# Three of four mask products in bfloat16, and three products of zeros between the first two chunks' attention, in an mLSTM cell followed by a squared-ReLU FFN

## The chip, the cores and the metric

The kernel runs on one core of one Trainium2 chip. The metric is the device time of one launch, in microseconds (us); lower is better. TensorE is called PE in the profile, its weight loads PEld, VectorE DVE, ScalarE ACT, GpSimdE POOL, and SyncE, which issues most DMAs, SP.

## The reference, cut to what matters

```python
# q, k, v, o_gate: (4, 8, 768, 40); i_gate, f_gate: (4, 8, 768); w_in: (320, 2048); w_out: (2048, 320)
for t in range(S):
    m_new = maximum(f[t] + m, i[t])
    f_stab, i_stab = exp(f[t] + m - m_new), exp(i[t] - m_new)
    m = m_new
    C = f_stab * C + i_stab * outer(v[t], k[t])          # 40 x 40 for each head
    n = f_stab * n + i_stab * k[t]
    y[t] = sigmoid(o[t]) * (C @ q[t]) / maximum(abs(n @ q[t]), 1.0)
x = y.transpose(0, 2, 1, 3).reshape(3072, 320)           # tokens x (heads * head_dim)
out = square(maximum(x @ w_in, 0.0)) @ w_out             # w_in, w_out arrive as float64
```

## The kernel before, in words

The recurrence is computed in chunks of 128 tokens: a sequence has 6 chunks, the four sequences 24, and the chunks are numbered s = 0 to 23 through all of them. Within a chunk the states are replaced by a masked matrix. For each of the 8 heads there is a matrix W of 128 key tokens (partitions) by 128 query tokens, W = exp(A + b), where A is a running sum of log decays that depends on the query token, b depends on the key token, and where the key comes after the query the entry must be zero. `do_gates` computes the running sums with scans on DVE (A_sb, line 251, and i_sb, line 255). `turn_gates` transposes them on PE, and ACT copies them out (b_T and eA_T, line 262).

Chunks 0 and 1 get their A from PE, by `spread_A(s)`: for each of two halves of four heads, a product of the identity with a matrix `later` (zero, or -1e30 where key is after query; line 346, 128x512 for four heads at once) starts a PSUM tile, and four products of a selecting matrix `sel` with A_sb (line 350) add A, spread over all partitions. These first products are here called the mask products; there are four, (s, i) = (0, 0), (0, 1), (1, 0), (1, 1). All later chunks read A back from DRAM with a broadcasting DMA (`load_A`), and POOL masks it (`mask`, line 359).

A chunk goes through these steps. `transposes` (line 412) turns k and q on PE, and copies them out on ACT or DVE (line 415). `scores` (line 424) multiplies them. `weigh` makes W on ACT (line 383), the decay of the state `dec` (line 387), and values-times-weight `vw` on POOL (line 396). `weighted` multiplies scores and W on DVE (line 437, into P_sb, for chunk 1 into r_sb). `attend` issues on PE the share of the old state `hi` (line 446), the new state `dC` (line 453), and the weights' product with the values `hp` (line 460); these three come from a pool of three PSUM banks, so the `hp` of chunk 1 goes into the bank of the `hp` of chunk 0 and waits until that is read. DVE then adds and normalises (`sum_of_h`, `normalise`; line 601 is the last to read `hp` of chunk 0), `turn_rows` transposes the result x on PE (line 633) and ACT copies it to xT (line 634).

The FFN takes two chunks at a time: `ffn1_main` and `ffn1_rest` (lines 649 and 660) multiply xT with w_in, ACT takes the ReLU (line 675) and DVE the square (line 682), and a second set of products with w_out follows. The weights arrive as float64 and are rounded to float32 by `Rounding`: `words` on ACT (lines 195 and 197), `join` with three steps on DVE (lines 206, 210, 211) and one on POOL (line 215), 26 pieces in all, whose loads SP issues as pieces are done.

The order of all this is written out by hand: each engine executes its instructions in the order in which the source issues them. `idle(n)` issues n products of zeros (line 802: bfloat16, 128x512) into a bank that nobody reads. The stretch around the change is

```python
    attend(0)
    rounding.step()
    sum_of_h(0)
    normalise(0)
    mask(2)
    attend(1)
```

and ahead of it stand `idle(12)`, `transposes(0, apart=4)`, `idle(4)`, `scores(0)`, `idle(3)`, `do_gates()`, `spread_A(0)`, `turn_gates()`, two joins, `weigh(0)`, `transposes(1)`, `spread_A(1)`, `scores(1)`, `weigh(1)`, and `weighted` for both. The tiles of the masks (`later`, `sel`, `keep`) lie in a pool that is freed after `weigh(1)`.

Of the kernel before, what the change touches and what calls it, by code (L numbers as in the profile page):

```python
# [12 lines left out]
BF16 = mybir.dt.bfloat16  # L13
# [4 lines left out]
P = 128  # L18
# [11 lines left out]
def kernel(  # L30
# [27 lines left out]
    nc = tc.nc  # L58
# [29 lines left out]
    gates = first.enter_context(tc.tile_pool(name="gates", bufs=1))  # L88
# [17 lines left out]
    ident = consts.tile([P, P], F32)  # L106
    bdm = conv.tile([P, PR, 2, D1], F32, bufs=1)
    keep = gates.tile([BH, NB, P], F32)
    sel = gates.tile([BH, H, P], F32)
    later = gates.tile([P, P], F32)  # L110

    w_in = consts.tile([P, 2, DFF], F32)
    w_in2 = consts.tile([P, NPAIR, P], F32)
# [2 lines left out]
    def make_consts():  # L116
        for t in kq_b:
            nc.vector.memset(t[:, :, :, D:], 0.0)
        for t in va_b:
            nc.vector.memset(t[:, :, D:], 1.0)  # L120
        nc.vector.memset(keep[:], 1.0)
        nc.vector.memset(keep[:, :, 0:1], 0.0)
        make_identity(nc, ident[:])

        nc.gpsimd.memset(sel[:], 0.0)
        nc.gpsimd.affine_select(
            sel[:], sel[:], compare_op=ALU.not_equal, fill=1.0, base=0, pattern=[[-1, H], [0, P]], channel_multiplier=1,
        )

        nc.gpsimd.memset(later[:], 0.0)  # L130
        nc.gpsimd.affine_select(
            later[:], later[:], compare_op=ALU.is_ge, fill=-1e30, base=0, pattern=[[1, P]], channel_multiplier=-1,
        )

        nc.gpsimd.memset(bdm[:], 1.0)
        nc.gpsimd.memset(bdm[:DP, :, 1, :], 0.0)
        nc.gpsimd.memset(bdm[DP:, :, 0, :], 0.0)
        for t in va_w:
            nc.gpsimd.memset(t[:, H * D1 :], 0.0)
# [189 lines left out]
    def load_A(s):  # L329
        b, c = divmod(s, NB)  # L330
        d = st.setdefault(s, {})
        A = ld.tile([P, H, P], F32, name="A_bc", bufs=2)
        d["A"] = [A]
        nc.sync.dma_start(
            A[:], bass.AP(A_d.tensor, A_d.offset + b * H * S + c * P, [[0, P], [S, H], [1, P]]),
        )

    def spread_A(s):

        b, c = divmod(s, NB)  # L340
        H2 = H // 2
        d = st.setdefault(s, {})
        d["A"] = []
        for i in range(2):
            A = ps_h.tile([P, H2, P], F32, name="A_ps", tag="h_ps")
            nc.tensor.matmul(
                A[:], lhsT=ident[:], rhs=later[:].unsqueeze(1).to_broadcast([P, H2, P]), start=True, stop=False,
            )
            for h in range(H2):
                nc.tensor.matmul(  # L350
                    A[:, h, :], lhsT=sel[:, i * H2 + h, :], rhs=A_sb[:, c * P : (c + 1) * P],
                    start=False, stop=(h == H2 - 1),
                )
            d["A"].append(A)

    def mask(s):

        A = st[s]["A"][0]
        nc.gpsimd.affine_select(  # L359
            A[:], A[:], compare_op=ALU.is_ge, fill=-1e30, base=0, pattern=[[0, H], [1, P]], channel_multiplier=-1,  # L360
        )
# [77 lines left out]
    def attend(s):  # L439
        b, c = divmod(s, NB)  # L440
        d = st[s]
        C = st.get("C")
        if c > 0:
            hi = ps_at.tile([P, H, D1], F32, name="hi", tag="at")
            for j in range(PR):
                nc.tensor.matmul(
                    hi[:, 2 * j : 2 * j + 2, :].rearrange("p h d -> p (h d)"), lhsT=d["qT"][:, j, :],
                    rhs=C[:, j].rearrange("p h d -> p (h d)"), start=True, stop=True,
                )
        if c + 1 < NB:  # L450
            dC = ps_at.tile([P, PR, 2, D1], F32, name="dC", tag="at")
            for j in range(PR):
                nc.tensor.matmul(
                    dC[:, j].rearrange("p h d -> p (h d)"),
                    lhsT=d["kq"][:, 0, 2 * j : 2 * j + 2, :].rearrange("p h d -> p (h d)"),
                    rhs=d["vw"][:, 2 * j : 2 * j + 2, :].rearrange("p h d -> p (h d)"), start=True, stop=True,
                )
        hp = d["hp"] = ps_at.tile([P, H, D1], F32, name="hp", tag="at")
        for h in range(H):
            nc.tensor.matmul(  # L460
                hp[:, h, :], lhsT=d["P"][h % 2][:, h // 2, :], rhs=d["va"][:, h, :], start=True, stop=True,
            )
        d["num"] = hp
        if c > 0:
            num = d["num"] = old.tile([P, H, D1], F32, name="num", bufs=1)
            nc.vector.tensor_tensor(
                num[:], hi[:], eA_T[:, b, c, :].unsqueeze(2).to_broadcast([P, H, D1]), op=ALU.mult,
            )
        if c + 1 < NB:
            Cn = old.tile([P, PR, 2, D1], F32, name="C_sb")  # L470
            nc.vector.tensor_tensor(Cn[:], dC[:], bdm[:], op=ALU.mult)
            if c > 0:
                Cd = old.tile([P, H, D1], F32, name="Cd", bufs=1)
                nc.gpsimd.tensor_tensor(
                    Cd[:], C[:].rearrange("p j i d -> p (j i) d"),
                    d["dec"][:].unsqueeze(2).to_broadcast([P, H, D1]), op=ALU.mult,
                )
                Cf = Cn[:].rearrange("p j i d -> p (j i) d")
                nc.gpsimd.tensor_tensor(Cf, Cf, Cd[:], op=ALU.add)
            st["C"] = Cn  # L480
# [104 lines left out]
    def sum_of_h(s):  # L585
        d = st[s]
        num = d["num"]
        if num is not d["hp"]:
            nc.vector.tensor_tensor(num[:], num[:], d["hp"][:], op=ALU.add)

    def normalise(s):
        d = st[s]
        num = d["num"]
        dm = work.tile([P, H], F32, name="dm")
        nc.vector.tensor_scalar(dm[:], num[:, :, D], scalar1=-1.0, scalar2=1.0, op0=ALU.mult, op1=ALU.max)
        nc.vector.tensor_tensor(dm[:], dm[:], num[:, :, D], op=ALU.max)
        nc.vector.reciprocal(dm[:], dm[:])

        x = d["x"] = work.tile([P, 3 * P], F32, name="x_sb")
        x3 = x[:, :DM].rearrange("p (h d) -> p h d", d=D)  # L600
        nc.vector.tensor_tensor(x3, num[:, :, :D], d["og"], op=ALU.mult)
        nc.vector.tensor_tensor(x3, x3, dm[:].unsqueeze(2).to_broadcast([P, H, D]), op=ALU.mult)
        nc.vector.tensor_copy(x[:, DM:], x[:, DM - KR : DM])
# [195 lines left out]
    def idle(n):  # L799
        t = ps_h.tile([P, W], F32, name="idle", tag="h_ps")  # L800
        for _ in range(n):
            nc.tensor.matmul(
                t[:], lhsT=zeros[:, :1].to_broadcast([P, P]), rhs=zeros[:, :1].to_broadcast([P, W]), start=True, stop=True,
            )
# [12 lines left out]
    load_part(0, 1)  # L817
    fetch(2)
    make_consts()
    load_part(1, 0)  # L820
    load_part(1, 1)
# [12 lines left out]
    rounding.words()  # L834
    nc.scalar.dma_start(A_d[:, :], A_sb[:])
    spread_A(0)
    rounding.words()
    turn_gates()
    rounding.join()
    rounding.join()  # L840
    weigh(0)
    transposes(1, (False, True))
    spread_A(1)
    scores(1, (True, True))
    weigh(1)
# [14 lines left out]
    sum_of_h(0)  # L860
    normalise(0)
    mask(2)
    attend(1)
    sum_of_h(1)
    normalise(1)
# [15 lines left out]
    for u in range(8):  # L881
        s = 2 + u // 2
# [118 lines left out]
    for n, (which, g, i) in enumerate(parts):  # L1001
        s, at = 6 + n // 4, n % 4
# [200 lines left out]
```

## Time and profile before

| | |
|---|---|
| time, median of 3 runs | 521.13 us (519.98 to 521.82) |
| time of the profiled execution | 521.13 us |
| span of the profiled execution, first to last instruction | 519.3 us |
| mean granted TensorE clock | 0.990 |
| busy: PE, DVE, ACT, POOL | 511.1, 333.9, 194.3, 91.0 us |

All times inside the kernel are us from the span's start in the profiled execution. A float32 product appears in the profile as two records, so "x8" on line 350 is four products. A granted clock of 1.00 is full speed. A group's duration reaches from the start of its first to the modelled end of its last record; the spacing of starts shows what a product costs in a row of them.

### The profile page before, as it was taken

How to read it: one execution, taken by the hardware profiler on the slowest of the kernel's cores; microseconds unless marked ns; L12 is line 12 of the kernel's file. 1: busy time of each engine (PE TensorE's matmuls, PEld its weight loads, DVE VectorE, ACT ScalarE, POOL GpSimd, SP SyncE). 2: the span in 40 equal slices, each digit the busy share in tenths (PEclk: the TensorE clock that was granted, in tenths of full speed). 3: DMA queues.
4: the chain of work that ended last, by engine and by line, in shares of the span. 5: the costliest groups of instructions: out<-in, count | busy, mean ns of one | idle time of the engine just before them, and what ended most of it. 6: DMA issues, size and time to landing. Idle time of an engine off the chain costs nothing.

```text
span 519.3 us, 10359 instructions
## 1 busy us (share of the span) xinstructions
PE 511.1 (98%) x3933; PEld 450.2 (87%) x3933; DVE 333.9 (64%) x638; ACT 194.3 (37%) x460; POOL 91.0 (18%) x110
## 2 busy tenths in 40 slices
PE   9999899999999999999999999999999999999997
PEld 4778788886698898998898898998898898998997
DVE  8669987857895574674864865764864863431461
ACT  3867468434454423532334423235432301103000
POOL 3345643222321111010210211110110000000000
PEclk9989799999999999999999999999999999999999
DMA  9997599867867768876775685686664221200000
GB/s 193 243 232 155 157 169 202 206 144 140 177 133 170 138 156 161 159 150 143 174 144 116 170 151 115 162 142 138 157 145 75 65 68 48 66 0 1 27 27 25
DMA packets 239394, 68.06 MB, mean 131 GB/s; under 512 B 185744, under 2 KB 233872, under 8 KB 239344
## 3 DMA queue, kind: packets, MB, share of 16 engines
q1 hardware_dynamic: 239248, 67.20, 60.2%
q8 instruction: 31, 0.51, 0.4%
q10 hardware_dynamic: 96, 0.20, 0.1%
q14 instruction: 19, 0.16, 0.1%
HBM read 55.08 MB, written 17.86 MB: 140 GB/s over the span
## 4 chain that ended last, share of the span: by engine, by line
PE 72%; DVE 2%; DMA 2%; issue 2%; SPq 1%; ACT 0%; DVEq 0%
PE h_ps L743 30%; PE h_ps L649 24%; PE h_ps L660 7%; PE numT L534 3%; PE tp L424 3%; PE h_ps L689 3%; PE numT L523 2%; DMA num_rows<-tn 1%; PE numT L512 1%; SPq L562 1%; DVE g L682 0%; DVE mag L210 0%; SPq L618 0%; DMA xT<-x_rows 0%; DMA kq<-num_rows 0%
## 5 line engine op out<-in xcount | busy, mean ns | idle before, releaser
L649 PE MATMUL h_ps<-xT,w_in 128*128 128x256 f32 x768 | 172.9, 383 | 1.4 <-ACT xT L634 0.6
L649 PEld LDWEIGHTS h_ps<-xT,w_in 128*128 128x128 f32 x768 | 144.4, 191 | 23.2 <-issue 1.4
L675 ACT ACTIVATE r_sb<-h_ps 128x512 f32<-128x512 f32 x96 | 50.5, 598 | 108.6 <-PE h_ps L660 52.9
L682 DVE TENSOR_TENSOR g<-r_sb 128x512 f32<-128x512 f32 x96 | 68.5, 762 | 12.0 <-ACT r_sb L675 11.9
L743 PE MATMUL h_ps<-w_out,g 128*128 128x160 f32 x528 | 75.5, 299 | 0.0
L743 PEld LDWEIGHTS h_ps<-w_out,g 128*128 128x128 f32 x528 | 72.9, 190 | 0.3 <-issue 0.2
L383 ACT ACTIVATE W_sb<-A_bc,b_T 128x128 f32<-128x128 f32 x176 | 53.8, 388 | 25.3 <-POOL A_bc L359 25.2
L437 DVE TENSOR_TENSOR P_sb<-tp,W_sb 128x512 f32<-128x512 f32 x46 | 29.7, 685 | 49.6 <-PE numT L534 32.3
L743 PE MATMUL h_ps<-T,S 128*128 128x160 f32 x352 | 52.3, 302 | 0.0
L743 PEld LDWEIGHTS h_ps<-T,S 128*128 128x128 f32 x352 | 48.8, 190 | 1.6 <-issue 0.9
L660 PE MATMUL h_ps<-xT,w_in 64*128 64x256 f32 x384 | 49.0, 391 | 0.0
L660 PEld LDWEIGHTS h_ps<-xT,w_in 64*128 64x128 f32 x384 | 34.8, 186 | 12.1 <-issue 8.8
L759 DVE TENSOR_TENSOR y_sb<-y_sb,h_ps 128x160 f32<-128x160 f32 x44 | 14.0, 319 | 42.9 <-PE h_ps L743 42.8
L359 POOL TENSOR_SCALAR_AFFINE_SELECT A_bc<-A_bc 128x1024 f32<-128x1024 f32 x22 | 27.2, 1236 | 71.4 <-ACT kq L369 65.1
L763 ACT COPY y_sb<-h_ps 128x160 f32<-128x160 f32 x11 | 3.2, 293 | 97.1 <-PE h_ps L743 97.1
L396 POOL TENSOR_TENSOR vw<-va,W_sb 128x328 f32<-128x328 f32 x20 | 18.7, 933 | 67.6 <-ACT W_sb L383 52.7
L316 DVE STREAM_TRANSPOSE kqT<-kqT 128x1024 f32<-128x1024 f32 x17 | 21.0, 1237 | 11.2 <-DMA kqT<-kq_rows 10.9
L490 POOL TENSOR_TENSOR Cd<-C,kq 128x164 f32<-128x164 f32 x15 | 7.0, 464 | 114.9 <-DVE C L551 99.5
L424 PEld LDWEIGHTS tp<-kqT 40*128 40x128 f32 x384 | 24.8, 188 | 2.4 <-issue 0.9
L369 ACT ACTIVATE kq<-A_bc 64x512 f32<-64x512 f32 x30 | 18.9, 629 | 20.4 <-DMA A_bc<-a_rows 18.6
L424 PE MATMUL tp<-kqT 40*128 40x128 f32 x384 | 26.1, 275 | 0.0
L743 PE MATMUL h_ps<-w_out,S 128*128 128x160 f32 x176 | 25.7, 299 | 0.0
(119 smaller groups left out, 605.1 us busy)
## 6 DMA issues: line engine op xcount, KB each, us to landing
A_bc<-a_rows SPq DMA_DIRECT2D x23, 512.0 KB, 5.0
raw<-in_moe_w_out_dram SPq DMA_DIRECT2D x16, 320.0 KB, 3.6
num_rows<-tn SPq DMA_DIRECT2D x18, 256.0 KB, 2.2
kq<-num_rows SPq DMA_DIRECT2D x72, 64.0 KB, 2.0
kqT<-kq_rows SPq DMA_DIRECT2D x34, 128.0 KB, 3.1
raw<-in_moe_w_in_dram SPq DMA_DIRECT2D x8, 512.0 KB, 5.3
kq<-in_k_dram SPq DMA_DIRECT2D x24, 160.0 KB, 3.8
va<-in_v_dram SPq DMA_DIRECT2D x24, 160.0 KB, 4.2
```

The source lines that it names most:

```text
L316: nc.vector.transpose(t, t)
L359: nc.gpsimd.affine_select(A[:], A[:], compare_op=ALU.is_ge, fill=-1e30, base=0, pattern=[[0, H], [1, P]], channel_multiplier=-1,)
L369: nc.scalar.activation(e[rows], st[s]["A"][0][rows, PR * i : PR * (i + 1), :], AF.Exp)
L383: nc.scalar.activation(d["W"][:, i * n + h, :], A[i][:, h, :], AF.Exp, bias=b_T[:, b, c, i * n + h : i * n + h + 1],)
L396: nc.gpsimd.tensor_tensor(d["vw"][:], d["va"][:], d["W"][:, :, P - 1 : P].to_broadcast([P, H, D1]), op=ALU.mult,)
L424: nc.tensor.matmul(sc[i][:, j, :], lhsT=d["kT"][rows, j, :], rhs=d["qT"][rows, j, :], start=True, stop=True,)
L437: nc.vector.tensor_tensor(t, d["sc"][i], d["W"][:, heads, :], op=ALU.mult)
L649: nc.tensor.matmul(hs[i][:, n, :], lhsT=w_in[:, a, fb * P : (fb + 1) * P], rhs=xT[:, :, a, :], start=(n == 0 and a == 0), stop=False,)
L660: nc.tensor.matmul(hs[i][:, n, :], lhsT=w_in2[rows, 2 * pp + n, :], rhs=xT[rows, :, 2, :], start=False, stop=(n == 1),)
L675: nc.scalar.activation(rs[-1][:], h[:], AF.Relu)
L682: nc.vector.tensor_tensor(g4[:, :, i, :], r[:], r[:], op=ALU.mult)
L743: nc.tensor.matmul(to, lhsT=lhsT[:, p], rhs=rhs[:, p, :], start=(start and p == 0), stop=(p == NPAIR - 1), skip_group_check=True,)
```

## The change

Two bfloat16 tiles are added, copies of the identity (made on ACT, behind the making of the identity on POOL) and of `later` (made on POOL, behind the making of `later`). Three of the four mask products, all but (s, i) = (1, 1), use these in place of the float32 ones; they still start the same float32 PSUM tiles, to which the float32 products of line 350 are added. And `idle(3)`, three products of zeros, is issued between `mask(2)` and `attend(1)`: on PE it stands behind the `hp` of chunk 0 and ahead of the `hi` of chunk 1. All other instructions keep their order on each engine.

```diff
@@ -108,6 +108,8 @@
     later = gates.tile([P, P], F32)
+    laterb = gates.tile([P, P], BF16)
+    identb = gates.tile([P, P], BF16)
@@ -121,6 +123,7 @@
         make_identity(nc, ident[:])
+        nc.scalar.copy(identb[:], ident[:])
@@ -131,6 +134,7 @@
         nc.gpsimd.affine_select(
             later[:], later[:], compare_op=ALU.is_ge, fill=-1e30, base=0, pattern=[[1, P]], channel_multiplier=-1,
         )
+        nc.gpsimd.tensor_copy(laterb[:], later[:])
@@ -343,8 +347,9 @@
             A = ps_h.tile([P, H2, P], F32, name="A_ps", tag="h_ps")
+            eye, low = (ident, later) if (s, i) == (1, 1) else (identb, laterb)
             nc.tensor.matmul(
-                A[:], lhsT=ident[:], rhs=later[:].unsqueeze(1).to_broadcast([P, H2, P]), start=True, stop=False,
+                A[:], lhsT=eye[:], rhs=low[:].unsqueeze(1).to_broadcast([P, H2, P]), start=True, stop=False,
             )
@@ -860,6 +865,7 @@
     normalise(0)
     mask(2)
+    idle(3)
     attend(1)
```

## The prediction

> **What bounds the kernel now.** I read the page first: the share of each engine, and the slices.
>
> ```profile
> PE 511.1 (98%) x3933; PEld 450.2 (87%) x3933; DVE 333.9 (64%) x638; ACT 194.3 (37%) x460; POOL 91.0 (18%) x110
> PEclk9989799999999999999999999999999999999999
> ```
>
> In the first fence line PE is busy for 98% of the span; the chain that ended last gives it 72%. So TensorE is the bound, and time is won only by giving it less work, fewer waits or a better clock. The clock is below 9 tenths in the third and the fifth slice of 13 us: the first 66 us are where the clock is lost, and the edit lies there too (9 to 26 us). So I read the timeline of that stretch next, whole lines of it (start, duration, engine, line, operation; in brackets the idle time before and who ended it):
>
> ```profile
> 8.45 1.75 DVE L251 TENSOR_TENSOR_SCAN A_sb<-keep,f_sb 32x768 f32<-32x768 f32 x1
> 8.98 0.82 PE L802 MATMUL idle<-zeros 128*128 128x512 bf16 x3
> 9.64 1.02 PE L346 MATMUL A_ps<-later,ident 128*128 128x512 f32 x2
> 10.59 1.15 PE L350 MATMUL A_ps<-A_sb,sel 32*128 32x128 f32 x8
> 11.67 1.12 PE L346 MATMUL A_ps<-later,ident 128*128 128x512 f32 x2
> 12.73 1.15 PE L350 MATMUL A_ps<-A_sb,sel 32*128 32x128 f32 x8
> 15.46 1.02 PE L346 MATMUL A_ps<-later,ident 128*128 128x512 f32 x2
> 16.41 1.15 PE L350 MATMUL A_ps<-A_sb,sel 32*128 32x128 f32 x8
> 17.50 1.13 PE L346 MATMUL A_ps<-later,ident 128*128 128x512 f32 x2
> 19.74 1.14 ACT L383 ACTIVATE W_sb<-A_ps,b_T 128x128 f32<-128x128 f32 x4 [0.93 <-PE A_ps L350]
> 21.00 1.29 DVE L437 TENSOR_TENSOR r_sb<-tp,W_sb 128x512 f32<-128x512 f32 x2 [2.83 <-ACT dec L387]
> 26.27 2.45 PE L460 MATMUL hp<-va,r_sb 128*128 128x41 f32 x16 [0.84 <-PE dC L453]
> 39.57 1.29 DVE L437 TENSOR_TENSOR P_sb<-tp,W_sb 128x512 f32<-128x512 f32 x2 [3.73 <-PE tp L424]
> 57.42 1.26 PE L453 MATMUL dC<-vw,kq 128*128 128x82 f32 x8 [1.38 <-DVE P_sb L437]
> ```
>
> The reader is to see a chain. From 10.6 to 23.4 us PE has no gap, and the four mask products (L346) stand in it, some 1.06 us each. The second half of chunk 1's decays leaves PE at 19.7; ACT waits 0.93 us for it; DVE waits 2.83 us for that. Then ACT's sigmoid and word extraction, DVE's rounding step and the normalising of chunk 0 (L601 ends at 25.72 + 0.44 = 26.16) follow without slack, and the product of chunk 1's weights with its values (L460, 26.27) waits for L601, because it reuses the bank that L601 reads. Lastly the PE clock, in stretches of 3.4 us:
>
> ```profile
> 20.80:24.20 3.40, 3.40 (x31) 1.00 1.08 158
> 24.20:27.60 3.40, 2.56 (x23) 0.99 1.01 229
> 27.60:31.00 3.40, 3.40 (x14) 0.51 1.02 247
> 31.00:34.40 3.40, 2.77 (x19) 1.00 1.31 195
> 54.90:58.30 3.40, 2.02 (x18) 0.99 0.32 100
> 58.30:61.70 3.40, 3.40 (x19) 0.50 0.31 82
> ```
>
> (Length; PE busy; granted clock; the DMA columns are not used.) The stretch with the 0.84 us wait has 2.56 us of PE work and is followed by a stretch at half clock; the one with the 1.38 us wait (2.02) by two. A stretch with 2.77 was followed by none.
>
> **The change, part by part.**
>
> *Mask products.* A float32 one costs PE 1.06 us (11.67 to 12.73), 0.95 (15.46 to 16.41) and, the first, 0.95 (9.64 to 10.59). No trace line shows a bfloat16 mask product, but the zeros (L802) have its shape and type: three take 8.98 to 9.64, so 0.22 us each. At half clock they are 0.43 us apart at the span's start: that is the upper bound. I take 0.22, as the clock is full here. The second product of chunk 0 then gives 1.06 - 0.22 = 0.84, the first of chunk 1 0.95 - 0.22 = 0.73. The first of all gives less: behind it L350 needs A_sb, which DVE ends at 8.45 + 1.75 = 10.20, so L350 moves from 10.59 to about 10.29, 0.30 us (bounds 0 and 0.73). Sum: 0.30 + 0.84 + 0.73 = **1.87 us**. The fourth product stays float32.
>
> *Is the 1.87 passed on?* Chunk 1's scores move from 19.64 to 17.77. They need two copies of transposed k and q. ACT's copy (16.98, 0.67 long) comes after chunk 0's decays and moves ahead with them, 1.14 us, to end at 16.5. DVE's copy (15.95, 0.68) stands behind the rounding of two pieces and stays, ending at 16.63. Both are early enough by over 1 us. The fourth product must wait until ACT has read chunk 0's first decays: that ends at 16.07 - 1.14 = 14.93, and the product now starts at 15.63. Values-times-weight on POOL (17.41, 0.73) stays and ends at 18.14; its first reader moves to 18.86. So ACT's last decays go from 19.74 to 17.87, DVE's r_sb from 21.00 to 19.13, and L601's end to 24.29.
>
> *The two conversions.* ident goes to bfloat16 on ACT, nearest row a copy of 128x384 in 0.48 us, bounds 0.1 and 0.59 (128x512); ACT is idle for 3.35 us before 5.82 and nothing there needs it. later goes on POOL: bounds 0.19 (its memset of 128x128) and 0.73 (the product of 128x328), taken at 0.3; the memsets behind it end at 5.07 and POOL then idles 8.64 us. Both results are wanted at 9.64. Cost nothing; without that cover their own 0.3 to 0.7 us.
>
> *Zeros ahead of chunk 1's attend.* Three of them, 3 x 0.22 = 0.66 us of PE, between hp of chunk 0 and hi of chunk 1. What queues behind them is hi, dC and hp of chunk 1; hp waits for L601 anyway, 0.84 us of it. So they fit into that wait and leave 0.18 us. They need a bank that ACT has released long before. If L601 came earlier than I think, they would cost up to 0.66.
>
> *The clock.* With 0.18 us of gap left, no stretch of 3.4 us here has below 3.2 us of PE work, against 2.56 before which the clock fell and 2.77 before which it did not. So by these rows the half clock of 27.6 to 31.0 goes. What it is worth: hp of chunk 1 takes 28.51 - 26.27 = 2.24 us, that of chunk 0 at full clock 23.43 - 21.68 = 1.75. From 28.51 on PE does the transpose of chunk 0's rows, four zeros, eight transposes, four zeros: 4.16 us to 32.67. At full clock that is 0.49 + 0.87 + 0.91 + 0.87 = 3.14, so PE could be there at 24.40 + 1.75 + 3.14 = 29.29. DVE's normalising of chunk 1 is the other arm: it began 0.24 us after hp's end, took from 28.75 to 31.83 = 3.08, and a start at 24.40 + 1.75 + 0.24 = 26.39 ends at 29.47. DVE is the later, so chunk 1's rows are transposed at about 29.5 in place of 32.67: **3.15 us** earlier in all, 1.87 of them from the products.
>
> The row is weighed against a rule here. The Trainium skill, "TensorE: Matmul & The Clock Gate", section "Why this matters for your kernels", says that the clock falls only after gaps of over about 3 us between bursts. The trace differs: 0.84 us and 1.38 us of waiting were followed by clocks of 0.51 and 0.50. By the rule the zeros would do nothing and the sum would be the first 1.87 alone; by the rows it is 3.15. I take the rows.
>
> *After that.* The first FFN block (33.79) follows at 30.6, chunk 2's scores and DVE's P_sb (39.57) at 36.4. DVE was idle 3.73 us before that line, so it is released by the path and can follow. From there to 57 us DVE is busy nearly throughout, and PE waits 1.38 us for it at 57.42; as its stretch starts from the shifted line, wait and half clock shift too, at the same size. Weight pieces and k, q, v landed some 5 us after their issue and issue follows DVE's steps. From 66 us to the end PE is busy 448.96 of 453 us at full clock, so the shift lasts.
>
> The profiled execution has a span of 519.3 us and a time of 521.13, which is also the median of the three runs. 521.13 - 3.15 = **518.0 us**.
>
> **The rivals.**
>
> *The half clock stays, the products' gain holds.* For it: the stretch at 58.3 to 61.7 was full of PE work and the clock still stayed low, so busy time is not the whole measure, and hp, hi and dC are small matmuls that fill this place. Time: 521.13 - 1.87 = 519.3.
>
> *DVE takes the gain.* Between 40 and 57 us DVE is nearly full; if its rounding is held by landings that do not move, PE arrives earlier and waits 1.38 + 3.15 us at 57. Against: the 3.73 us that DVE idles. Time about 521.1.
>
> *Slower: the clock gate.* The products replaced are dense PE work, 0.95 to 1.06 us each, in a stretch whose rest is small matmuls; and everything later falls elsewhere in the gate's stretches. A stretch at half clock costs up to 1.7 us. If two more fall (one near 20 to 24 us, where 3.40 of 3.40 us were busy before, one after the wait at 57), the time is 521.13 - 1.87 + 3.4 = 522.7. It decides from the second such stretch on. Against: the three zeros stand at just this place.
>
> *One cold stretch less after 57 us* (one in place of two), from the new position of that wait: 518.0 - 1.7 = 516.3.
>
> **How the numbers follow.** My forecast 0.45, half clock stays 0.25, DVE takes it 0.12, slower 0.13, one less 0.05. A difference under 0.3% (1.56 us, so 519.57 to 522.69) is about what a measurement of this kernel can't tell from no change. Faster: 0.45 + 0.05, and 0.17 of the 0.25, as 519.3 is near the bound: 0.67. Same: 0.08 + 0.12 = 0.20. Slower 0.13. The range, 516.8 to 521.4, holds the first three cases and the spread of the three runs, and leaves out the last two.
>
> **What would show it.** Three mask products at about 0.22 us spacing and one at 1.06; chunk 1's decays on ACT near 17.9; hp of chunk 1 near 24.4 with a wait below 0.3; no half clock near 24 to 31; the first FFN block near 30.6; the wait of 1.4 us near 54 with its half clock. Wrong, if the first FFN block starts after 32.5, or if it is early and the wait at 54 to 57 has grown by as much, or if clocks of 0.5 stand at new places.

## The result, and the profile after

| | kernel before | changed kernel |
|---|---|---|
| median | 521.09 us of 4 runs (519.98 to 521.82) | 517.65 us of 4 runs (516.92 to 530.37) |
| profiled execution: time, span | 521.13, 519.3 us | 517.84, 516.0 us |
| mean granted clock | 0.990 | 0.993 |

The ratio is 0.9931, 95% interval [0.9907, 0.9956]: 3.4 us less by the medians, where 3.15 were forecast. All ratios here leave out executions that lie over 1.5% above the fastest of their kernel and ran at a lower clock (the 530.37, at 0.968, is one); medians and ranges include them.

The clock line of the page of the changed kernel, 40 slices of 12.9 us:

```profile
PEclk9999799999999999999999999999999999999999
```

The dip of the third slice has gone; that of the fifth has stayed. The timeline of the changed kernel, the same steps as shown of before (line numbers are some 5 higher):

```profile
8.40 1.75 DVE L255 TENSOR_TENSOR_SCAN A_sb<-keep,f_sb 32x768 f32<-32x768 f32 x1
9.69 0.38 PE L351 MATMUL A_ps<-laterb,identb 128*128 128x512 bf16 x1
10.20 1.15 PE L355 MATMUL A_ps<-A_sb,sel 32*128 32x128 f32 x8
11.29 0.39 PE L351 MATMUL A_ps<-laterb,identb 128*128 128x512 bf16 x1
11.61 1.15 PE L355 MATMUL A_ps<-A_sb,sel 32*128 32x128 f32 x8
14.34 0.38 PE L351 MATMUL A_ps<-laterb,identb 128*128 128x512 bf16 x1
14.64 1.15 PE L355 MATMUL A_ps<-A_sb,sel 32*128 32x128 f32 x8
15.73 1.12 PE L351 MATMUL A_ps<-later,ident 128*128 128x512 f32 x2
17.97 1.14 ACT L388 ACTIVATE W_sb<-A_ps,b_T 128x128 f32<-128x128 f32 x4 [0.35 <-PE A_ps L355]
19.23 1.29 DVE L442 TENSOR_TENSOR r_sb<-tp,W_sb 128x512 f32<-128x512 f32 x2 [1.46 <-ACT dec L392]
24.49 1.95 PE L465 MATMUL hp<-va,r_sb 128*128 128x41 f32 x16 [0.27 <-PE dC L458]
28.02 1.26 DVE L607 TENSOR_TENSOR x_sb<-x_sb,dm 128x320 f32<-128x320 f32 x1
36.65 1.29 DVE L442 TENSOR_TENSOR P_sb<-tp,W_sb 128x512 f32<-128x512 f32 x2 [2.18 <-PE tp L429]
54.53 1.12 PE L458 MATMUL dC<-vw,kq 128*128 128x82 f32 x8 [1.39 <-DVE P_sb L442]
```

The reader is to see the whole chain move by 1.8 us up to hp of chunk 1 (26.27 to 24.49) and by 2.9 from P_sb of chunk 2 on (39.57 to 36.65), and the later wait of PE for DVE move along with its size kept, 1.38 to 1.39. The clock in stretches (length; PE busy; granted clock; DMA columns not used):

```profile
20.80:24.20 3.40, 3.40 (x29) 1.00 1.04 156
24.20:27.60 3.40, 3.13 (x25) 1.00 1.02 237
27.60:31.00 3.40, 2.63 (x17) 1.00 1.08 250
51.40:54.90 3.50, 2.11 (x19) 1.00 0.33 108
54.90:58.30 3.40, 3.40 (x21) 0.60 0.14 26
58.30:61.70 3.40, 3.40 (x15) 0.50 1.03 274
```

Full clock in the rows up to 54.9; the half clock after the second wait is still there, two stretches of it as before.

### The profile page after: what moved, and what is told of

Read it like the earlier page. It is cut to its first block, busy times and chain, and to the rows that moved or that the text cites. A ratio compares the mean times of both kernels' runs of the same rounds, so it can differ in the third digit from the quotient of the medians.

```text
span 516.0 us, 10360 instructions
## 1 busy us (share of the span) xinstructions
PE 508.5 (99%) x3933; PEld 448.9 (87%) x3933; DVE 335.9 (65%) x638; ACT 194.1 (38%) x461; POOL 92.1 (18%) x111
## 4 chain that ended last, share of the span: by engine, by line
PE 88%; DVE 6%; DMA 3%; issue 2%; ACT 1%; POOL 0%; SPq 0%; DVEq 0%; ACTq 0%; POOLq 0%
PE h_ps L748 32%; PE h_ps L654 29%; PE h_ps L665 8%; PE tp L429 4%; PE numT L539 3%; PE h_ps L694 3%; PE hp L465 2%; PE numT L528 2%; PE numT L517 1%; DMA kq<-in_k_dram 1%; PE tp L417 1%; PE dC L458 1%; DVE g L687 1%; PE A_ps L355 1%; PE hi L451 1%
## 5 line engine op out<-in xcount | busy, mean ns | idle before, releaser
L748 PE MATMUL h_ps<-T,g 128*128 128x160 f32 x176 | 25.7, 299 | 0.0
```

Of the source, the lines that this page charges most:

```text
L748: nc.tensor.matmul(to, lhsT=lhsT[:, p], rhs=rhs[:, p, :], start=(start and p == 0), stop=(p == NPAIR - 1), skip_group_check=True,)
```

## The experiments

My theory was that the products are worth some 1.9 us by the chain, and the zeros some 1.3 by the clock. The rivals were that the zeros do nothing (the gate needs longer gaps) and that they do it all. One execution's profile says little of 1 us here, since the kernels' starts differ by as much (see the end), so within a profile I count from the start of the first mask product (`idle` to `spread_A`, line 346 or 351) to that of the first FFN block (line 649 or 654): 9.64 to 33.79 = 24.15 us before, 9.69 to 30.87 = 21.18 us changed, a gain of 2.97. (The second profile of the changed kernel, shown further on, gives 10.17 to 31.43 = 21.26.)

**The products alone.**

```diff
     mask(2)
-    idle(3)
     attend(1)
```

> The three bfloat16 mask products without the three zeros. Theory (the products are worth some 1.9 us by the chain, the zeros keep the clock, worth some 1.3): 519.2 us, hp of chunk 1 starts near 24.4 as in the changed kernel but after a wait of some 0.9 us, and half clock comes back for one stretch of 3.4 us between 24 and 31. Rival A (the gate needs gaps of 3 us, so the zeros do nothing): 517.7, full clock from 5 to 53 us. Rival B (the zeros did all of it): 521.

Measured: ratio 0.9976 [0.9955, 0.9997], 12 runs. Profile, the wait of hp of chunk 1 and the stretches around it:

```profile
25.53 1.95 PE L465 MATMUL hp<-va,r_sb 128*128 128x41 f32 x16 [0.84 <-PE dC L458]
23.80:27.20 3.40, 2.56 (x24) 1.00 1.02 224
27.20:30.60 3.40, 3.18 (x14) 0.53 1.06 247
```

The wait of 0.84 us and the half clock behind it are back. The anchored stretch is 10.94 to 33.02 = 22.08, a gain of 2.07 us where 1.87 were forecast; over the kernel the interval allows 0.2 to 2.3 us. Rival A would have full clock here; in this profile it falls.

**The zeros alone**, in the kernel before.

```diff
     mask(2)
+    idle(3)
     attend(1)
```

> The three zeros in the kernel before, all mask products in float32. Theory: hp of chunk 1 starts at 26.3 as before, its wait shrinks from 0.84 to some 0.2 us, the half clock between 27.6 and 31 goes, and the first FFN block starts near 32.6 instead of 33.8: 519.8 us. Rival A (zeros do nothing): 521.1. Rival B (zeros did all of it): 517.8.

Measured: ratio 0.9963 [0.9933, 0.9994], 12 runs.

```profile
27.46 1.95 PE L460 MATMUL hp<-va,r_sb 128*128 128x41 f32 x16 [0.27 <-PE dC L453]
23.80:27.20 3.40, 3.34 (x27) 1.00 0.90 219
27.20:30.60 3.40, 2.83 (x22) 1.00 1.01 246
```

The wait is 0.27 us, the clock is full, the anchored stretch is 10.83 to 33.83 = 23.00, a gain of 1.15 where 1.28 were forecast. Both rivals fall: each half has its part, and 2.07 + 1.15 = 3.22 against 2.97 for both together. Over the whole kernel the ratios put the zeros ahead of the products, but the intervals overlap, so the shares are known from the profiles only. That the zeros act on the clock, and not in one profile alone, shows in the mean clock of the single executions: it is 0.992 or more in 1 of 12 with the products alone, in 8 of 12 with the zeros alone, in 9 of 10 of the changed kernel, and in 23 of 74 of the kernel before. So they keep it in most executions and not in all, and the kernel before keeps it in some without them.

**All four products in bfloat16.**

```diff
-            eye, low = (ident, later) if (s, i) == (1, 1) else (identb, laterb)
+            eye, low = identb, laterb
```

> The changed kernel with the fourth mask product in bfloat16 too. Theory: PE is there 0.84 us earlier, but ACT's decays of chunk 1's first half end only 0.35 us before the second half now starts, so the chain moves by 0.35 us alone and the wait of hp of chunk 1 grows from 0.3 to some 0.8 us: 517.3 us if the clock holds, near 518.6 if a stretch of half clock follows that wait as it did in the kernel before. Rival (PE's work alone sets the chain): 516.8.

Measured: 0.9987 [0.9949, 1.0026], 12 runs, three of them outside the ratio at 0.970 or 0.971. The nine in it are of two kinds. Six took 519.15 to 520.83 at a mean clock of 0.989 or 0.990, lower than the changed kernel's 0.993 by about what one stretch of half clock makes; their median is 1.7 us below that of before (522.06), where the second forecast, 518.6, was 2.5 below. Three took 524.51 to 525.80 at 0.977, and the profiled execution is one of these:

```profile
10.20:13.60 3.40, 3.40 (x31) 1.00 1.08 213
13.60:17.00 3.40, 3.40 (x16) 0.53 1.12 159
17.00:20.40 3.40, 3.40 (x16) 0.50 0.91 260
23.80:27.20 3.40, 3.40 (x17) 0.50 0.95 166
27.20:30.60 3.40, 3.18 (x14) 0.50 1.06 238
```

The clock is half from 13.8 to 30.9, though PE waits for no other engine there, and the first FFN block starts at 37.15. No execution of a kernel with the fourth product in float32 had 0.977 (a few had 0.968 to 0.974; they are counted at the end). This is what the slower rival of the prediction forecast, in a kernel one product further on; its reason is not shown by it. What made the clock fall at 13.8 lies ahead of the fourth product (17.40), where this kernel and the changed one have the same PE work, so in this execution the fourth product can only matter for how long it stays low.

**Another product left in float32.**

```diff
-            eye, low = (ident, later) if (s, i) == (1, 1) else (identb, laterb)
+            eye, low = (ident, later) if (s, i) == (0, 1) else (identb, laterb)
```

> The changed kernel with the second half of chunk 0 in float32 in place of the second half of chunk 1. PE has the same work, but ACT's decays of chunk 0 start 0.84 us later and ACT, with 0.35 us of slack before chunk 1's last decays, ends some 0.5 us later. Theory: 518.2 us, 0.5 above the changed kernel, if the clock holds in both; and its dense work is back between 10 and 14. Rival (only PE's sum counts): 517.65.

Measured: ratio 0.9938 [0.9905, 0.9972]; 12 runs, 7 of them outside the ratio at the mean clock of 0.977 (their times, 524.86 to 526.18, are those of the long half clock above; none of them has a profile). The profiled execution (518.25) has hp of chunk 1 at 24.76 against 24.49 and the FFN block at 31.14 against 30.87: 0.3 us later where 0.5 were forecast. So as long as the clock holds the choice costs a few tenths; that it held in fewer executions was not expected, and goes against the idea that dense work between 10 and 14 is what protects it. Three products are in bfloat16 here as in the changed kernel, so their number does not decide it either.

**Dense zeros ahead of the first two products.**

```diff
             A = ps_h.tile([P, H2, P], F32, name="A_ps", tag="h_ps")
+            for _ in range({(0, 0): 1, (0, 1): 2}.get((s, i), 0)):
+                nc.tensor.matmul(A[:].rearrange("p h t -> p (h t)"), lhsT=zeros[:, :1].to_broadcast([P, P]),
+                    rhs=zeros[:, :1].to_broadcast([P, W]), start=True, stop=True)
```

> The changed kernel with three more zeros of 0.22 us ahead of the first two mask products (one in PE's wait for A_sb, two in PE's way). Theory (half clock from 13.8 on, which the kernel with all four products in bfloat16 showed over 17 us, comes from a stretch that the short products left too sparse): the zeros cost 0.44 us where the clock holds, 518.1 us against 517.65, and their runs spread less, none with a half clock from 14 to 31. Rival (the spread comes from elsewhere): the same spread and 0.44 us more.

Measured: 0.9951 [0.9925, 0.9976]; the changed kernel beside it, in six more runs, 0.9941 [0.9918, 0.9964]:

> The changed kernel once more, on the chip of the three kernels beside it and with more runs. Theory: 0.993 of the kernel before, as measured first. Rival (the first result was a favourable place of the gate's stretches): 0.996 or nearer to 1.

The first result is confirmed. The zeros' 0.44 us are within what the intervals allow; the spread did not shrink (516.13 to 521.65 in the ratio, one outside it at 529.94). The rival holds here. This profile also refutes a reading of mine:

```profile
27.20:30.60 3.40, 3.08 (x21) 1.00 0.88 220
30.60:34.00 3.40, 1.90 (x9) 1.00 1.37 178
34.00:37.40 3.40, 3.40 (x24) 1.00 1.11 243
```

PE is busy for 1.90 of 3.40 us, less than in any stretch that was followed by half clock, and the clock stays full. (The stretches are laid by me; no row says where the gate's own begin.) PE waits 1.25 us there, until 31.53, and in the second profile of the changed kernel it waits longer still:

```profile
31.43 3.72 PE L654 MATMUL h_ps<-xT,w_in 128*128 128x256 f32 x16 [1.40 <-ACT xT L639]
30.60:34.00 3.40, 2.57 (x12) 1.00 1.28 215
34.00:37.40 3.40, 3.40 (x33) 1.00 1.08 231
```

No half clock follows, where 0.84 us before hp of chunk 1 was enough. So the length of a wait does not decide it alone. What stands around it may: here the FFN's wide products come next, there small ones; no run separates this from the place in time.

**Four in bfloat16, and dense zeros ahead of the fourth.** The loop of the kernel above, with `{(1, 1): 3}`, added to the kernel with all four.

> All four mask products in bfloat16, with three dense zeros (0.66 us) ahead of the fourth, so that PE streams there about as long as with the float32 product. Theory D (all four lost to half clock from 13.8 on because this place had become sparse): no run at a mean clock of 0.977, 0.994 of the kernel before, as the changed kernel. Rival (the float32 product matters for another reason, or the loss is a matter of the earlier arrival): the spread of all four stays, 0.9987, with runs at 0.977.

Measured: 0.9933 [0.9905, 0.9962], 11 runs, of which four stand outside the ratio, one of them at 0.977 and three near 0.971. The seven in the ratio are as the changed kernel's. But this ratio leaves its execution at 0.977 out, where that of all four holds three of them, and four long losses in 11 speak against the theory, which expected none. Why the fourth product matters is not settled.

**Narrow zeros in the wait.**

```diff
-    idle(3)
+    t_sp = ps_h.tile([P, W], F32, name="idle", tag="h_ps")
+    for _ in range(12):
+        nc.tensor.matmul(t_sp[:, :32], lhsT=zeros[:, :1].to_broadcast([P, P]),
+            rhs=zeros[:, :1].to_broadcast([P, 32]), start=True, stop=True)
```

> The changed kernel with twelve narrow products of zeros (32 columns each, some 0.06 us with their weight load) in place of the three of 512 columns: PE is as long busy in the wait of chunk 1, but streams 384 columns in place of 1536. Theory D (the gate goes by how densely PE streams, not by whether it waits): the half clock after that wait comes back in many runs, time as with the products alone, 0.9976 of the kernel before, mean clock 0.989 to 0.990. Theory B (the gate goes by waits): 0.993 to 0.994 of before, mean clock 0.993, as in the changed kernel.

Measured: 0.9937 [0.9913, 0.9961], 7 runs; mean clock 0.993 or better in five, 0.989 and 0.990 in two.

```profile
21.66 0.46 PE L870 MATMUL idle<-zeros 128*128 128x32 bf16 x12
21.97 1.10 PE L451 MATMUL hi<-C_sb,kqT 128*128 128x82 f32 x8
24.49 1.95 PE L465 MATMUL hp<-va,r_sb 128*128 128x41 f32 x16 [0.52 <-PE dC L458]
23.80:27.20 3.40, 2.82 (x23) 1.00 0.98 222
27.20:30.60 3.40, 2.77 (x18) 1.00 0.98 237
```

The twelve took 0.31 us in a row (21.66 to 21.97), not the 0.66 I had worked with, so they fill about half of the 0.84 us and leave 0.52. Even so the clock holds in this profile, and the time is the changed kernel's within the intervals. That density is the whole measure is not what this shows, though the two executions at 0.989 and 0.990 have no like among the nine of the changed kernel in its ratios; whether a shorter wait or a later one is what counts stays open.

**Zeros in the second wait.** In `attend`, behind the products of `hi`:

```diff
+        if s == 3:
+            idle(6)
```

> The changed kernel with six more zeros (1.3 us) on PE between hi and dC of chunk 3, in the wait of 1.39 us at 53.1 to 54.5. Theory (a short wait beside small matmuls drops the clock): the half clock from 55.8 to 62.6 goes or is halved. hp, the transposes and the FFN block there take some 3 us more than at full clock, so 514.7 if PE alone sets the end of this stretch, 516.5 if DVE, busy throughout there, gives only half of it. Rival (the clock falls for another reason, or DVE sets that stretch anyway): 517.7, with half clock or with a longer wait after it.

Measured: 0.9899 [0.9864, 0.9933], 9 runs, two of them outside the ratio at 0.971; profiled span 515.3. Stretches after the wait, and two later waits on PE:

```profile
54.40:57.80 3.40, 3.40 (x33) 1.00 0.19 18
57.80:61.20 3.40, 3.40 (x18) 1.00 1.01 273
170.79 1.26 PE L429 MATMUL tp<-kqT 40*128 40x128 f32 x16 [1.26 <-issue]
190.09 7.17 PE L656 MATMUL h_ps<-xT,w_in 128*128 128x256 f32 x32 [0.70 <-DVE xT L632]
```

The half clock is gone (mean clock 0.999 to 1.000 in all executions of the ratio). The last long FFN block before 120 us starts at 105.08 instead of 107.98, 2.90 us earlier. Of this 0.36 was there ahead of the zeros' effect (dC of chunk 3 starts at 54.17 and not at 54.53), so the zeros gave 2.5 of the 3 that PE alone would give. The span is shorter by 0.7 only: in this execution 1.26 + 0.70 us went into two later waits that the changed kernel's profile does not have.

**Both kinds of zeros**, twice.

> The zeros of the last two kernels together: three ahead of the first two mask products, six in the wait of chunk 3. Theory: 0.44 us above the kernel with the six alone where that one keeps full clock, so near 517.3 us, with fewer runs that lose the clock early, so the lowest mean of all. Rival: nothing is won over the six zeros alone.

> The changed kernel with three zeros ahead of the first two mask products and six in the wait of chunk 3, once more. Theory: full clock from 5 us to the end in most runs, 0.992 of the kernel before, below the changed kernel's 0.9941. Rival: the first result was luck, 0.994 or more.

Measured: 0.9922 [0.9901, 0.9943], 6 runs, and 0.9925 [0.9895, 0.9955], 8 runs, one of them outside the ratio at 0.974. The first profile has full clock to the end and a span of 513.6 us, the shortest of the profiles. Against the changed kernel (0.9931 and 0.9941) this version and the one with the six zeros alone (0.9899) are better by the point, but every interval overlaps; that they beat it is likely and not shown.

## Why the prediction was right

*The mask products.* Forecast 0.30 + 0.84 + 0.73 = 1.87 us. Measured, by the starts of the steps behind them: 10.59 to 10.20, then spacings of 0.32 and 0.30 in place of 1.06 and 0.95, so 0.39 + 0.74 + 0.65 = 1.78 us. The 0.22 us from the zeros' row was too little by 0.1 each time: a bfloat16 product costs more between float32 ones than in a row of its own kind. No run shows why.

*Passing it on.* As forecast: ACT's last decays at 17.97 (forecast 17.87), hp of chunk 1 at 24.49 (24.40). ACT's wait for PE ahead of its last decays shrank from 0.93 to 0.35 us, as PE comes earlier by more than ACT does.

*The conversions* took 0.30 us on ACT (from 2.48) and 0.29 on POOL (from 3.92), and nothing waited for them.

*The zeros* left a wait of 0.27 us (forecast 0.18), and the half clock of 27.6 to 31.0 went; the two experiments with one half each, and the clocks counted there, show it.

*DVE as the later arm.* Right in kind, mis-sized: chunk 1's normalising ends at 29.31 + 0.61 = 29.92, not 29.47. It started 0.09 us later than forecast and took 3.44 us, not 3.08. L607 took 1.26 us where the step took 0.49 before, and L608 0.61 in place of 0.20, while two steps that had stood beside POOL's work before got shorter (0.49 to 0.17 and 0.94 to 0.44). POOL's mask of chunk 2 waits for a DMA, and lies at 27.66 to 28.93 now, beside L607; before, it came at 27.95, ahead of these steps. The second profile of the changed kernel has the mask later, and there L607 takes 0.49 again. The step and the mask in before, in the changed kernel and in its second profile:

```profile
27.95 1.09 POOL L359 TENSOR_SCALAR_AFFINE_SELECT A_bc<-A_bc 128x1024 f32<-128x1024 f32 x1 [1.23 <-DMA A_bc<-a_rows]
31.10 0.49 DVE L602 TENSOR_TENSOR x_sb<-x_sb,dm 128x320 f32<-128x320 f32 x1
27.66 1.27 POOL L364 TENSOR_SCALAR_AFFINE_SELECT A_bc<-A_bc 128x1024 f32<-128x1024 f32 x1 [2.71 <-DMA A_bc<-a_rows]
28.30 0.49 DVE L607 TENSOR_TENSOR x_sb<-x_sb,dm 128x320 f32<-128x320 f32 x1
29.51 1.25 POOL L364 TENSOR_SCALAR_AFFINE_SELECT A_bc<-A_bc 128x1024 f32<-128x1024 f32 x1 [4.29 <-DMA A_bc<-a_rows]
```

I had moved DVE and forgotten what POOL would do beside it. So the FFN block is at 30.87, not 30.6, and the gain there 2.92, not 3.15. In the second profile ACT's copy of xT comes late instead (30.91, behind a sigmoid that waits for a DMA), so the block is no earlier there.

*After that* the shift held: 2.92 at 36.65, 2.88 at the blocks of 67.66 (70.54) and 107.98 (110.86). The spans differ by 3.3; the last 0.4 are later waits of PE (0.4 for xT and 0.1 for P_sb more before, 0.3 for S more after, and the rest too small to name), so part of the good agreement is luck: a shortfall of 0.2 at the FFN block and later waits of 0.4 happen to go opposite ways.

*What was wrong in the argument:* the reading that half clock follows a stretch with PE busy for 2.56 of 3.40 us and not one with 2.77. Stretches with 2.63 (changed kernel) and 1.90 were not followed by it, and the forecast that no stretch here would have below 3.2 failed too (3.13 and 2.63). The rule of the Trainium skill against which it was set ("TensorE: Matmul & The Clock Gate", "Why this matters for your kernels": against drops of the clock, no idle gaps of over about 3 us between bursts) does not fit either: 0.84 us was enough twice. The prediction drew its conclusion, that the zeros keep the clock, from that threshold. So the conclusion holds, by the experiments, but the reason given for it does not, and this part of the hit was in part luck. Smaller: of the four mask products only three stand in the stretch from 10.6 to 23.4 us; the first is at 9.64.

*The rivals.* DVE did not take the gain: its wait kept its size. The half clock of chunk 1 did not stay, and behind the second wait there are still two stretches of it. The slower rival was right that a clock can be lost early for long, and the changed kernel has such an execution itself (530.37). Its reason, dense work taken away, is not shown: dense zeros put back did not stop it.

## What to carry to other kernels

Work out a gain along the chain from one engine to the next, and look at each step for what does not move with it: a landing, or another engine's long instruction that now falls beside it. A short wait in front of small matmuls can cost more through TensorE's clock than by itself (0.84 us of waiting, and 0.90 to 1.15 us more behind it by the profiles), and zeros in that wait are nearly free. Not every wait does: 1.40 us ahead of wide products did not. Taking work from TensorE can cost the clock as well, so the granted clock of several executions belongs beside each time.

## What the runs showed of the hardware that was not expected

*The start is a lottery of 1.3 us.* The first twelve zeros are 0.43 us apart, their spacing at half clock, until the clock comes on. That happens between 3.5 and 3.8 us in the profile of before, near 4.3 in that of the changed kernel, and after all twelve in the profiles of the two halves, whose first transposes come at 6.02 us instead of 5.15 and 5.23. Their first mask products stand at 10.94 and 10.83, not at 9.64. The Trainium skill ("TensorE: Matmul & The Clock Gate", "What's actually happening") describes activity windows of 3.4 us that run on their own, not from the kernel's start; the half clocks here, which begin at 27.6 (before), 13.8 (all four) and 55.6 us (changed kernel) and last 3.4, 17.1 and 6.8 us, fit that. My sum set one execution against another that happened to start alike (9.64 and 9.69).

*The clock can stay half while PE waits for nothing.* With all four products short it did so for 17 us. Neither PE's busy time, nor the length of a wait, nor the density of one filling explains when; what the gate measures stays open.

*The fourth product's type goes with how often the clock is lost for long.* A mean clock of 0.977 or less stands in 17 of 35 executions of the three kernels that have it in bfloat16, in 5 of 64 of those with it alone of the four in float32 (1 of 10 of the changed kernel), and in none of 86 with all four in float32. Why stays open; for the changed kernel it means that an execution now and then gives back more than the change gains.
